# Seven chunks of weights instead of five have their bits assembled during attention

## The chip, the cores and the metric

The kernel runs on one core of a Trainium2 chip. The metric is the device time of one execution in microseconds. Before the change the median of 3 runs is 726.2 us (725.83 to 726.29).

## What is computed

Four batches of eight heads of attention over 576 positions, with a bias from a small MLP over relative positions, are followed by a feed-forward network (FFN) over the 2304 tokens.

```python
scores = scale * np.matmul(q, k.transpose(0, 1, 3, 2))
x = (psi_rel / psi_i)[..., None]
bias = np.maximum(x @ w1 + b1, 0.0) @ w2
scores = scores + bias.transpose(2, 0, 1)[None, :, :, :]
attn = softmax(scores)
x = (attn @ v).transpose(0, 2, 1, 3).reshape(B * S, H * D)
h = x @ w_in
out = np.maximum(0.01 * h, h) @ w_out
```

All inputs are float32 except the two weight matrices `w_in` (512 x 2048) and `w_out` (2048 x 512), which are float64. The kernel reads each of their elements as two 32-bit words and assembles a float32 from the bits.

## The kernel before

**Stages.** The bias is generated first (some 60 us). Then come 16 units of attention, one per pair of heads and batch, numbered 0 to 15; a unit has nine tiles, i = 0 to 8 (A0, B0, A1, B1, M, A2, B2, A3, B3), of 128 rows of scores each. Then the FFN runs over 4 blocks of 512 tokens and a last one of 256; in each block it goes through 16 chunks m of 128 hidden columns.

**Engines.** PE does all matmuls in float32r. `step(n)` issues tile n: its scores on PE (`qk_mm`, line 230) into one of two PSUM tiles `ps_s`, a DVE operation that adds the bias and takes the maximum (line 252), the transposes of the tile three before (line 295) and their evacuation on ACT (line 311), and the exponential on ACT (line 260). The context product of a unit's halves (`pv`, line 335) is issued in the steps i = 0 and i = 4 of the next unit. Its result is scaled on DVE (lines 344 and 348). For the first batch of each pair of heads, which belongs to FFN block 0, it is also split into a high and a low part: a cast on ACT (line 345) and a subtraction on DVE (line 360). These splits fall into units 1, 5, 9 and 13.

**Splits for float32r.** Each float32 operand is a high part (rounded by a copy into float32r) and a low part (the rest); three products make one. `split_hi` does it for q and k of the next unit on DVE (lines 192 and 197), `split_lo` the rest on GpSimd (POOL; lines 204 and 207).

**The weights.** Chunk m has two halves, one of `w_in` (called wi) and one of `w_out` (wo). A half passes through these functions:

- `w_fill` (line 394) loads its raw words into one of three buffers `raw` through SP's queue;
- `w_abs` (line 400, ACT) writes the high word without its sign into a tile `tmp`: **abs** below;
- `w_bits` k = 0 to 3 (DVE, lines 407, 409, 411, 413) clamps, shifts and masks, takes over the sign bits, and takes over three bits of the low word: **clamp, shift, sign, low** below. The last one frees the raw buffer and calls `w_fill`;
- `w_hi` (line 419, ACT) casts to the high part, and `w_lo` (line 423, DVE) subtracts it: **cast** and **residual**.

For chunks 0 to 4 abs to low are done during attention (for chunk 0 also cast and residual). A list `early_ops` is filled at n = 13, and from unit 2 on two of its operations are taken after the steps i = 0 and i = 4: **slot 0** and **slot 4** of a unit. The tiles `tmp` of chunks 0 to 2 rotate through four buffers in pool `stage`; chunks 3 and 4 have four more in `stage_y`.

```python
for _ in range({0: 2, 4: 2}.get(i, 0) if n >= 18 else 0):
    if early_ops:
        f, *args = early_ops.pop(0)
        f(*args)
```

**The FFN's work list.** The remaining weight work is in `todo`, each entry with a cost. In each FFN iteration j, `ffn1` of chunk j is issued on PE, then `work(2.6)`, then two activations on ACT (`ffn_act`, lines 449 and 450, into `gh` and `g`), `work(2.6)` again, the low part `gl` on DVE (`ffn_lo`, line 456), and `ffn2` of chunk j - 2 on PE (lines 467 to 469), whose third product per token tile reads `gl`. `work` takes entries until their costs reach its budget: clamp 0.42, shift 0.43, sign, low and residual 0.69 each, ACT's entries 0.

Of the kernel before, what the change touches and what calls it, by code (L numbers as in the profile page):

```python
# [8 lines left out]
F32 = mybir.dt.float32  # L9
# [6 lines left out]
DM, DFF = 512, 2048  # L16
# [3 lines left out]
MF = DFF // 128  # L20
HS = S // 2
S0 = 512 - HS
PIT = S + 32
KW = 2 * S + 64
KINDS = ["A0", "B0", "A1", "B1", "M", "A2", "B2", "A3", "B3"]
GEN = [16, 17] + list(range(16)) + [34, 35] + list(range(18, 26)) + list(range(33, 25, -1))
SPL = {0: [(0, "q")], 1: [(1, "q", 0)], 3: [(1, "q", 1)], 4: [(0, "k")], 5: [(1, "k", 0)], 7: [(1, "k", 1)]}
# [8 lines left out]
def attention_ffn(ctx: ExitStack, tc: tile.TileContext, qt, kt, vm, vt, wi, wo, cst, out):  # L36
    nc = tc.nc
    PS = bass.MemoryType.PSUM
    xp = ctx.enter_context(tc.tile_pool(name="xp", bufs=1))
# [10 lines left out]
    def pstile(tag):  # L50
        shape = [128, 1024] if tag == "s" else [128, 512]
        return ps.tile(shape, F32, tag=tag, name="ps_" + tag)

    raw_b = [[ap.tile([128, c], F32, name=f"raw{c}{i}") for c in (2 * S, KW)] for i in range(2)]
    ident = ap.tile([128, 128], F32, name="ident")
    make_identity(nc, ident[:])
# [131 lines left out]
    def split_hi(u, what):  # L188
        q_, k_ = raw[u]
        if what == "q":  # L190
            qs = qs_b[u % 2]
            nc.vector.tensor_copy(qs[:].rearrange("p (a c) -> p a c", a=2)[:, :, 0:S], q_[:].rearrange("p (a c) -> p a c", a=2))
            ks1 = ap.tile([128, KW], F32R, tag="ks1", name="ks1", bufs=2)
            ks2 = ap.tile([128, KW], F32R, tag="ks2", name="ks2", bufs=2)
            qk[u] = (qs, ks1, ks2)
# [3 lines left out]
    def split_lo(u, what, a):  # L199
# [5 lines left out]
        else:  # L205
            c = slice(S * a, KW if a else S)
            nc.gpsimd.tensor_sub(ks2[:, c], k_[:, c], ks1[:, c].bitcast(F32))
# [3 lines left out]
    def tile_id(n):  # L211
        u, i = divmod(n, 9)
        return u, KINDS[i]

# [21 lines left out]
    def softmax_a(n):  # L236
        u, kind = tile_id(n)
        hp = u // B
        bt = bias[hp, "M"][:] if kind == "M" else bias[hp, kind[1]][:, 0 if kind[0] == "A" else 1, :]
        col = 1 if kind[0] == "B" else 0  # L240
        if col == 0:
            mx_t[n] = ap.tile([128, 2], F32, tag="mx", name="mx", bufs=6)
            sm_t[n] = ap.tile([128, 4], F32, tag="sm", name="sm", bufs=6)
        else:
            mx_t[n], sm_t[n] = mx_t[n - 1], sm_t[n - 1]
        if kind == "M":
            pair[0] = ap.tile([128, S + 64], F32, tag="pM", name="pM", bufs=1)
        elif col == 0:
            pair[0] = ap.tile([128, 2 * S], F32, tag="p", name="p", bufs=3)
        p = pair[0][:, S * col:S * col + S]  # L250
        s_, i = st.pop(n), mx_t[n][:, col:col + 1]
        nc.vector.tensor_tensor_reduce(out=p, in0=s_[:, S0:S0 + S], in1=bt, scale=-0.125, scalar=3.4e38, op0=ALU.add, op1=ALU.min, accum_out=i)  # L252
        pp[n] = pair[0]
        ex_q.append((p, i, sm_t[n][:, col:col + 1]))
# [97 lines left out]
    def step(n):  # L352
        if n < NTILE:
            qk_mm(n)
            softmax_a(n)
        if 0 <= n - 1 < NTILE and KINDS[(n - 1) % 9][0] != "A":
            recip(n - 1)
# [12 lines left out]
    pools = {}  # L370
# [25 lines left out]
            nxt[0] += 1  # L396

    def w_abs(m, i):
        y = pools["y" if m in (3, 4) else "s"].tile([128, DM], F32, tag="tmp", name="tmp", bufs=4)
        nc.scalar.activation(out=y[:], in_=raws[m, i][:, :, 1].bitcast(F32), func=AF.Abs)  # L400
        tmps[m, i] = y

# [76 lines left out]
    with tc.manual_schedule():  # L479
        gen_setup()  # L480
        for u in range(2):
            load_unit(u)
            load_v(u)
        sp_ops = [(u, w, a) for u in range(1) for w, a in (("q", None), ("q", 0), ("q", 1), ("k", None), ("k", 0), ("k", 1))]
        done = -1
        early_ops = []
        for n in range(NTILE + LAG + 6):
            u, i = divmod(n, 9)
            if u == 0:
                while done < GEN_AT[i]:  # L490
                    gen_tick(done)
                    done += 1
                    if done >= 6 and done % 2 == 0 and sp_ops:
                        w = sp_ops.pop(0)
                        split_hi(*w[:2]) if w[2] is None else split_lo(*w)
            if n == 8:
                gen.close()
                early = ctx.enter_context(tc.tile_pool(name="early", bufs=1, side="right"))
                x_alloc(early, 0)
                w_alloc(early, 0)  # L500
                early.tile([128, 24], F32, name="gap")
                stage, stage_y = ExitStack(), ExitStack()
                pools["s"] = stage.enter_context(tc.tile_pool(name="stage", bufs=1, side="right"))
                pools["y"] = stage_y.enter_context(tc.tile_pool(name="stage_y", bufs=1, side="right"))
            step(n)
            if n == 13:
                w_fill()
                for m in range(5):
                    early_ops += [(w_abs, m, h) for h in range(2)]
                    early_ops += [(w_bits, m, h, k) for k in range(4) for h in range(2)]  # L510
                    if m == 0:
                        early_ops += [(w_hi, 0, h) for h in range(2)] + [(w_lo, 0, h, nc.vector) for h in range(2)]
            for _ in range({0: 2, 4: 2}.get(i, 0) if n >= 18 else 0):
                if early_ops:
                    f, *args = early_ops.pop(0)
                    f(*args)
            if n == NTILE + 2:
                ffn1(0, 0)
            if u < HP * B:
                if u % B == B - 1 and u // B + 1 < HP:  # L520
                    c = {1: "0", 2: "1", 3: "M", 4: "2", 6: "3"}.get(i)
                    if c:
                        load_bias(u // B + 1, c)
                if u + 1 < HP * B:
                    for f, *args in SPL.get(i, ()):
                        (split_hi, split_lo)[f](u + 1, *args)
                if i == 0 and u + 2 < HP * B:
                    load_unit(u + 2)
                if i == 8 and u + 2 < HP * B:
                    load_v(u + 2)  # L530
        att.close()
        fp = ctx.enter_context(tc.tile_pool(name="ffn", bufs=1, reuse_waits="tile"))
        for m in range(1, MF - 1):
            w_alloc(fp, m)
        for c in ("g", "gh", "gl"):
            gt[c] = [fp.tile([128, BLK], F32 if c == "g" else F32R, name=f"{c}{i}") for i in range(1 if c == "g" else 3)]
        w_split(1)

        def more():
            stage_y.close()  # L540
            w_alloc(ctx.enter_context(tc.tile_pool(name="last", bufs=1, reuse_waits="tile")), MF - 1)

        todo = []
        for m in range(2, 5):
            todo += [(0, w_hi, m, i) for i in range(2)] + [(0.69, w_lo, m, i, nc.vector) for i in range(2)]
        todo.append((0, more))
        halves_ = [(m, i) for m in range(5, MF) for i in range(2)]
        todo += [(0, w_abs, *t) for t in halves_[:2]]
        for j, t in enumerate(halves_):
            todo += [(0.42, w_bits, *t, 0), (0.43, w_bits, *t, 1)]  # L550
            if j:
                todo.append((0.69, w_lo, *halves_[j - 1], nc.vector))
            todo += [(0.69, w_bits, *t, 2), (0.69, w_bits, *t, 3)]
            todo.append((0, w_hi, *t))
            if j + 2 < len(halves_):
                todo.append((0, w_abs, *halves_[j + 2]))
        todo.append((0.69, w_lo, *halves_[-1], nc.vector))

        def work(budget):
            while todo and budget > 0:  # L560
                cost, f, *args = todo.pop(0)
                f(*args)
                budget -= cost

        seq = [(n, m) for n in range(len(BLOCKS)) for m in range(MF)]
        for j in range(len(seq) + 2):
            if j < len(seq):
                n, m = seq[j]
                if j:
                    ffn1(n, m)  # L570
                work(2.6)
                ffn_act(n, m)
                work(2.6)
                ffn_lo()
                if (n, m) == (0, MF - 3):
                    assert not todo
                    stage.close()
                    lp = ctx.enter_context(tc.tile_pool(name="late", bufs=1, side="right", reuse_waits="tile"))
                    x_alloc(lp, 1)
                    x_split(1, 0)  # L580
                if n + 1 < len(BLOCKS) and m >= MF - (4 if n else 3):
                    x_split(n + 1, m - MF + 4)
            if j >= 2:
                ffn2(*seq[j - 2])
# [41 lines left out]
```

## Time and profile before

| | us |
|---|---|
| median of 3 runs | 726.2 |
| the profiled execution | 725.89 |
| its span | 723.7 |
| PE busy | 703.4 (97%) |
| DVE busy | 394.2 (54%) |
| ACT busy | 365.7 (51%) |
| POOL busy | 127.0 (18%) |

A matmul counts as busy from its start to its modelled end, and matmuls overlap, so PE's share is an upper view of its work. An idle stretch is shown in brackets with what ended it. Instructions that follow each other closely on one engine and line are merged into one row with their count. The granted clock of TensorE is 1.00 of 2.4 GHz nearly throughout.

### The profile page before, as it was taken

The numbers are of one execution on the slowest core, as the hardware profiler recorded it, in microseconds if no ns is written. First come the engines' busy times: TensorE is split into PE (matmuls) and PEld (weight loads), VectorE is DVE, ScalarE is ACT, GpSimd is POOL, SyncE is SP. The second block draws the span as 40 slices with busy tenths as digits, with TensorE's granted clock in tenths as the row PEclk, the third lists the DMA queues.
The fourth block names the chain that finished last, engine by engine and source line by source line (L and its number), as shares of the span: only waits on it lengthen the run. The fifth ranks groups of instructions, "written<-read, shape, count | busy, mean of one in ns | idle before, by whom it ended". The sixth has DMA issues, their size and how long they took to land.

```text
span 723.7 us, 11398 instructions
## 1 busy us (share of the span) xinstructions
PE 703.4 (97%) x4192; PEld 556.7 (77%) x4192; DVE 394.2 (54%) x1012; ACT 365.7 (51%) x808; POOL 127.0 (18%) x167
## 2 busy tenths in 40 slices
PE   6899999999999999998999999999999999999998
PEld 2347788778877887776777888888888888888996
DVE  7997789789888889759998211112111221112111
ACT  7797777777868677764555231132221231122221
POOL 2104545445544444300000000000000000000000
PEclk9999999999999999999999999999999999999999
DMA  9798848537626960103552010000100010000100
GB/s 222 241 314 244 224 109 242 129 88 216 188 69 164 249 172 18 59 1 120 175 175 83 1 58 1 1 0 1 58 1 1 0 59 1 0 1 0 59 1 30
DMA packets 30263, 68.26 MB, mean 94 GB/s; under 512 B 8192, under 2 KB 8320, under 8 KB 30208
## 3 DMA queue, kind: packets, MB, share of 16 engines
q1 hardware_dynamic: 30208, 67.54, 32.9%
q8 instruction: 33, 0.54, 0.3%
q14 instruction: 22, 0.18, 0.1%
HBM read 51.92 MB, written 15.61 MB: 93 GB/s over the span
## 4 chain that ended last, share of the span: by engine, by line
PE 80%; DVE 16%; issue 1%; DMA 1%; ACT 1%; SPq 0%; DVEq 0%
PE ps_o L441 11%; PE ps_t L441 11%; PE ps_o L335 10%; PE ps_s L230 10%; PE ps_s L469 8%; PE ps_s L467 8%; PE ps_s L468 8%; PE ps_t L295 7%; DVE p L252 2%; PE ps_o L123 2%; DVE tmp L411 2%; PE ps_t L123 2%; DVE tmp L413 2%; DVE r L112 2%; DVE wol L423 1%
## 5 line engine op out<-in xcount | busy, mean ns | idle before, releaser
L456 DVE TENSOR_TENSOR gl<-g,gh 128x512 fp32r<-128x512 f32 (+1 forms) x80 | 51.0, 638 | 263.9 <-ACT g L450 263.9
L230 PE MATMUL ps_s<-ks,qs 128*128 128x288 f32 x640 | 120.2, 314 | 3.1 <-DVE mx L252 3.1
L469 PE MATMUL ps_s<-woh,gl 128*128 128x512 f32 x288 | 112.9, 392 | 1.9 <-DVE gl L456 1.9
L467 PE MATMUL ps_s<-woh,gh 128*128 128x512 f32 x288 | 112.5, 390 | 1.6 <-ACT g L450 1.6
L468 PE MATMUL ps_s<-wol,gh 128*128 128x512 f32 x288 | 112.3, 390 | 0.0
L252 DVE CUSTOM_DVE_ANT_0 p<-ps_s,bias 128x576 f32<-128x576 f32 x128 | 95.0, 751 | 24.3 <-PE ps_s L230 23.6
L260 ACT ACTIVATE p<-p,mx 128x576 f32<-128x576 f32 x128 | 99.9, 780 | 11.3 <-DVE mx L252 10.4
L230 PEld LDWEIGHTS ps_s<-ks,qs 128*128 128x128 f32 x640 | 89.4, 189 | 18.8 <-DVE mx L252 5.0
L311 ACT COPY PT<-ps_t 128x512 f32<-128x512 f32 x128 | 73.7, 576 | 37.5 <-PE ps_t L295 37.5
L449 ACT ACTIVATE gh<-ps_o 128x512 fp32r<-128x512 f32 (+1 forms) x39 | 21.5, 552 | 124.4 <-PE ps_o L441 124.4
L295 PE MATMUL ps_t<-ident,p 128*128 128x128 f32 x512 | 76.9, 273 | 0.9 <-ACT PT L311 0.8
L449 ACT ACTIVATE gh<-ps_t 128x512 fp32r<-128x512 f32 (+1 forms) x39 | 21.5, 552 | 111.1 <-PE ps_t L441 111.0
L335 PE MATMUL ps_o<-PT,v 128*64 128x288 f32 x512 | 69.2, 412 | 0.0
L469 PEld LDWEIGHTS ps_s<-woh,gl 128*128 128x128 f32 x288 | 54.0, 188 | 16.2 <-DVE gl L456 5.0
L467 PEld LDWEIGHTS ps_s<-woh,gh 128*128 128x128 f32 x288 | 54.2, 188 | 12.6 <-ACT g L450 2.0
L295 PEld LDWEIGHTS ps_t<-ident,p 128*128 128x128 f32 x512 | 61.7, 140 | 2.7 <-ACT PT L311 1.8
L468 PEld LDWEIGHTS ps_s<-wol,gh 128*128 128x128 f32 x288 | 54.2, 188 | 10.6
L441 PE MATMUL ps_t<-xh,wil 128*128 128x512 f32 (+1 forms) x156 | 57.3, 367 | 0.0
L441 PE MATMUL ps_o<-xh,wil 128*128 128x512 f32 (+1 forms) x156 | 57.3, 367 | 0.0
L441 PE MATMUL ps_t<-xl,wih 128*128 128x512 f32 (+1 forms) x156 | 57.3, 367 | 0.0
L441 PE MATMUL ps_o<-xl,wih 128*128 128x512 f32 (+1 forms) x156 | 57.3, 367 | 0.0
L441 PE MATMUL ps_o<-xh,wih 128*128 128x512 f32 (+1 forms) x156 | 57.3, 367 | 0.0
(98 smaller groups left out, 1114.5 us busy)
## 6 DMA issues: line engine op xcount, KB each, us to landing
raw<-kt SPq DMA_DIRECT2D x32, 304.0 KB, 5.8
raw<-qt SPq DMA_DIRECT2D x32, 288.0 KB, 5.2
raw<-wi SPq DMA_DIRECT2D x16, 512.0 KB, 3.6
raw<-wo SPq DMA_DIRECT2D x16, 512.0 KB, 3.6
scr<-x SPq DMA_DIRECT2D x21, 295.5 KB, 4.0
bias<-scr SPq DMA_DIRECT2D x16, 288.0 KB, 5.3
out<-x SPq DMA_DIRECT2D x18, 256.0 KB, 2.1
v<-vm SPq DMA_DIRECT2D x16, 256.0 KB, 4.1
```

Of the source, the lines that this page charges most:

```text
L230: nc.tensor.matmul(s_[:, S0 + HS * hh:S0 + HS * hh + HS], qs[:, c0:c0 + 128], ks[:, k0 + HS * hh:k0 + HS * hh + HS], start=(j == 0), stop= ...
L252: nc.vector.tensor_tensor_reduce(out=p, in0=s_[:, S0:S0 + S], in1=bt, scale=-0.125, scalar=3.4e38, op0=ALU.add, op1=ALU.min, accum_out=i)
L260: nc.scalar.activation(out=p, in_=p, func=AF.Exp, bias=i, scale=-1.0, accum_out=sm)
L295: nc.tensor.transpose(t0[:, 128 * jb:128 * jb + 128], p[:, p0 + 128 * jb:p0 + 128 * jb + 128], ident[:])
L311: nc.scalar.copy(out=PT[u, g][:, 0:8, c].rearrange("p (j h) c -> p j h c", h=2)[:, :, h, :], in_=t0[:].rearrange("p (j c) -> p j c", j=4))
L335: nc.tensor.matmul(o[64 * h:64 * h + 64, 0:HS], l, r, start=(jb == 0), stop=(jb == 4))
L441: nc.tensor.matmul(h_[:, :N], w, x[:, :N], start=(j == 0), stop=(j == len(mms) - 1))
L449: nc.scalar.activation(out=gh[:, :N], in_=h_[:, :N], func=AF.Prelu, alpha=0.01)
L456: nc.vector.tensor_sub(gl[:, :N], g[:, :N], gh[:, :N].bitcast(F32))
L467: nc.tensor.matmul(o, gh[:, c], wt[m][2][:], start=(m == 0), stop=False)
L468: nc.tensor.matmul(o, gh[:, c], wt[m][3][:], start=False, stop=False)
L469: nc.tensor.matmul(o, gl[:, c], wt[m][2][:], start=False, stop=(m == MF - 1))
```

## The change

The number of chunks whose bits are assembled during attention goes from 5 to 7. Their four additional tiles are allocated in a pool that lasts (`xp`), named `y50` to `y61`; the room is taken from the area for dynamic DMA descriptors, 2048 bytes per partition in place of the default. The slots take three operations each. In the FFN's list the casts and residuals of chunks 5 and 6 stand where those of chunks 2 to 4 do, ahead of the first abs, which is now that of chunk 7.

```diff
+EARLY = 7
...
+    tmp_x = {(m, i): xp.tile([128, DM], F32, name=f"y{m}{i}") for m in range(5, EARLY) for i in range(2)}
...
     def w_abs(m, i):
-        y = pools["y" if m in (3, 4) else "s"].tile([128, DM], F32, tag="tmp", name="tmp", bufs=4)
+        if (m, i) in tmp_x:
+            y = tmp_x[m, i]
+        else:
+            y = pools["y" if m in (3, 4) else "s"].tile([128, DM], F32, tag="tmp", name="tmp", bufs=4)
...
-                for m in range(5):
+                for m in range(EARLY):
...
-            for _ in range({0: 2, 4: 2}.get(i, 0) if n >= 18 else 0):
+            for _ in range({0: 3, 4: 3}.get(i, 0) if n >= 18 else 0):
...
-        for m in range(2, 5):
+        for m in range(2, EARLY):
             todo += [(0, w_hi, m, i) for i in range(2)] + [(0.69, w_lo, m, i, nc.vector) for i in range(2)]
-        todo.append((0, more))
-        halves_ = [(m, i) for m in range(5, MF) for i in range(2)]
+            if m == 4:
+                todo.append((0, more))
+        halves_ = [(m, i) for m in range(EARLY, MF) for i in range(2)]
...
-    nc = bacc.Bacc("TRN2", target_bir_lowering=False, num_devices=1)
+    nc = bacc.Bacc("TRN2", target_bir_lowering=False, num_devices=1, dynamic_dma_scratch_size=2048)
```

What the slots hold, where it matters below:

| unit | slot 0 before | slot 0 now | slot 4 before | slot 4 now |
|---|---|---|---|---|
| 2 | abs abs | abs abs clamp | clamp clamp | clamp shift shift |
| 3 | shift shift | sign sign low | sign sign | low cast cast |
| 5 | residual residual | shift shift sign | abs abs | sign low low |
| 6 | clamp clamp | abs abs clamp | shift shift | clamp shift shift |
| 7 | sign sign | sign sign low | low low | low abs abs |
| 9 | shift shift | low low abs | sign sign | abs clamp clamp |
| 11 | clamp clamp | abs abs clamp | shift shift | clamp shift shift |
| 12 | sign sign | sign sign low | low low | low abs abs |
| 13 | abs abs | clamp clamp shift | clamp clamp | shift sign sign |
| 14 | shift shift | low low | sign sign | none |
| 15 | low low | none | none | none |

DVE's order at slot 0 of unit 7 before. L265 and L266 belong to the reciprocal of the row sums, L192 is the cast of q, L252 the softmax operation of the next tile.

```order
L265 TENSOR_SCALAR sm<-sm 128x2
L266 RECIPROCAL sm<-sm 128x2
L411 SCALAR_TENSOR_TENSOR tmp<-raw,tmp 128x512 x2
L192 CAST qs_96<-raw_78 128x2x576
L252 ISA p,mx<-ps_s,bias 128x576
```

The same place with the change; the source lines are 2 to 5 higher.

```order
L267 TENSOR_SCALAR sm<-sm 128x2
L268 RECIPROCAL sm<-sm 128x2
L416 SCALAR_TENSOR_TENSOR tmp<-raw,tmp 128x512 x2
L418 SCALAR_TENSOR_TENSOR tmp<-raw,tmp 128x512
L194 CAST qs_100<-raw_82 128x2x576
L254 ISA p,mx<-ps_s,bias 128x576
```

A low operation now stands between the two signs and the cast of q.

DVE's order at slot 4 of unit 13 before, where L197 is the cast of k.

```order
L252 ISA pM,mx<-ps_s,biasM 128x576
L252 ISA mx 128x1
L265 TENSOR_SCALAR sm<-sm 128x2
L266 RECIPROCAL sm<-sm 128x2
L407 TENSOR_SCALAR tmp<-tmp 128x512 x2
L197 CAST ks_3767<-raw_79 128x1216
L252 ISA p,mx<-ps_s,bias 128x576
```

And with the change; y_80 and y_81 are two of the four new tiles.

```order
L254 ISA pM,mx<-ps_s,biasM 128x576
L254 ISA mx 128x1
L267 TENSOR_SCALAR sm<-sm 128x2
L268 RECIPROCAL sm<-sm 128x2
L414 TENSOR_SCALAR y_81<-y_81 128x512
L416 SCALAR_TENSOR_TENSOR y_80<-raw,y_80 128x512
L416 SCALAR_TENSOR_TENSOR y_81<-raw,y_81 128x512
L199 CAST ks_3802<-raw_83 128x1216
L254 ISA p,mx<-ps_s,bias 128x576
```

Two clamps have become a shift and two signs.

DVE's order before the first `gl` of the FFN, before the change (the residuals wil and wol of chunk 4, then the bits of chunk 5).

```order
L423 TENSOR_TENSOR wil_4463<-tmp,wih_4462 128x512
L423 TENSOR_TENSOR wol_4465<-tmp,woh_4464 128x512
L407 TENSOR_SCALAR tmp<-tmp 128x512
L409 TENSOR_SCALAR tmp<-tmp 128x512
L411 SCALAR_TENSOR_TENSOR tmp<-raw,tmp 128x512
L456 TENSOR_TENSOR gl_4510<-g_4506,gh_4507 128x512
L413 SCALAR_TENSOR_TENSOR tmp<-raw,tmp 128x512
```

With the change, from the residuals of chunk 4 on.

```order
L428 TENSOR_TENSOR wil_4495<-tmp,wih_4494 128x512
L428 TENSOR_TENSOR wol_4497<-tmp,woh_4496 128x512
L428 TENSOR_TENSOR wil_4499<-y_78,wih_4498 128x512
L428 TENSOR_TENSOR wol_4501<-y_79,woh_4500 128x512
L461 TENSOR_TENSOR gl_4542<-g_4538,gh_4539 128x512
L428 TENSOR_TENSOR wil_4503<-y_80,wih_4502 128x512
L428 TENSOR_TENSOR wol_4505<-y_81,woh_4504 128x512
L412 TENSOR_SCALAR tmp<-tmp 128x512
```

Ahead of the first `gl` the residuals of chunk 5 have taken the place of three operations on its bits; the first clamp, of chunk 7, comes after the residuals of chunk 6.

## Rows read from the trace of the kernel before

**Rows 1.** Stretches: length, busy us of PE, PEld, DVE, ACT, POOL, then granted clock.
```profile
160.00:200.00 40.00, 40.00 (x322) 32.90 (x320) 33.94 (x104) 29.94 (x72) 19.72 (x26) 1.00 0.66 184
...
330.00:350.00 20.00, 18.31 (x79) 14.86 (x80) 19.66 (x39) 11.95 (x21) 0.00 (x0) 1.00 0.53 162
```

**Rows 2.** Timeline of PE: last matmuls of context products (start, us, engine, line, operation).
```profile
169.38 0.66 PE L335 MATMUL ps_o<-PT,vt 128*64 128x288 f32 x4
...
185.24 0.66 PE L335 MATMUL ps_o<-PT,vt 128*64 128x288 f32 x4
...
208.95 0.66 PE L335 MATMUL ps_o<-PT,vt 128*64 128x288 f32 x4
...
218.72 0.66 PE L335 MATMUL ps_o<-PT,vt 128*64 128x288 f32 x4
...
274.15 0.66 PE L335 MATMUL ps_o<-PT,vt 128*64 128x288 f32 x4
...
283.62 0.66 PE L335 MATMUL ps_o<-PT,vt 128*64 128x288 f32 x4
```

**Rows 3.** Timeline of DVE and PE, unit 7, slot 0 and after slot 4.
```profile
169.06 1.36 DVE L411 SCALAR_TENSOR_TENSOR tmp<-raw,tmp 128x512 int32<-128x512 int32 x2
170.34 0.75 DVE L192 CAST qs<-raw 128x1152 fp32r<-128x1152 f32 x1
171.01 0.75 DVE L252 CUSTOM_DVE_ANT_0 p<-ps_s,bias 128x576 f32<-128x576 f32 x1
...
172.14 0.76 PE L230 MATMUL ps_s<-ks,qs 128*128 128x288 f32 x4
...
178.39 0.76 DVE L252 CUSTOM_DVE_ANT_0 p<-ps_s,bias 128x576 f32<-128x576 f32 x1 [0.70 <-PE ps_s L230]
```

**Rows 4.** Who waited for whom, 310 to 400 us (us in total, times, longest).
```profile
PE ps_s L469 <- DVE gl L456: 1.9, 7, 0.6
```

**Rows 5.** Timeline of DVE and PE in the FFN's first block.
```profile
323.01 0.68 DVE L423 TENSOR_TENSOR wil<-tmp,wih 128x512 fp32r<-128x512 f32 x1
...
329.35 0.68 DVE L456 TENSOR_TENSOR gl<-g,gh 128x512 fp32r<-128x512 f32 x1
...
383.59 0.50 PE L469 MATMUL ps_s<-woh,gl 128*128 128x512 f32 x1 [0.23 <-DVE gl L456]
...
389.52 0.50 PE L469 MATMUL ps_s<-woh,gl 128*128 128x512 f32 x1 [0.20 <-DVE gl L456]
```

**Rows 6.** The chain that ended last, FFN (start, us, what).
```profile
392.08 2.72 PE ps_o L441 x12
```

**Rows 7.** Timeline of DVE and PE, slots of units 9 and 13.
```profile
202.53 0.76 DVE L252 CUSTOM_DVE_ANT_0 p<-ps_s,bias 128x576 f32<-128x576 f32 x1 [0.24 <-PE ps_s L230]
...
208.70 1.36 DVE L411 SCALAR_TENSOR_TENSOR tmp<-raw,tmp 128x512 int32<-128x512 int32 x2
...
209.54 0.79 PE L230 MATMUL ps_s<-ks,qs 128*128 128x288 f32 x4
...
210.69 0.74 DVE L252 CUSTOM_DVE_ANT_0 p<-ps_s,bias 128x576 f32<-128x576 f32 x1
...
273.91 0.84 DVE L407 TENSOR_SCALAR tmp<-tmp 128x512 f32<-128x512 f32 x2
...
274.66 0.78 DVE L197 CAST ks<-raw 128x1216 fp32r<-128x1216 f32 x1
274.74 0.79 PE L230 MATMUL ps_s<-ks,qs 128*128 128x288 f32 x4
...
275.57 0.76 DVE L252 CUSTOM_DVE_ANT_0 p<-ps_s,bias 128x576 f32<-128x576 f32 x1
```

**Rows 8.** Timeline of ACT: abs pair in unit 8, exponential in unit 9.
```profile
185.67 1.21 ACT L400 ACTIVATE tmp<-raw 128x512 f32<-128x512 f32 x2
...
208.76 0.77 ACT L260 ACTIVATE pM<-pM,mx 128x576 f32<-128x576 f32 x1
```

**Rows 9.** DMA issues on the page: name, queue, count, KB each, us to landing.
```profile
raw<-wi SPq DMA_DIRECT2D x16, 512.0 KB, 3.6
```

## Prediction

> **What bounds the kernel now.** I read the busy time of two stretches first. In 160 to 200 us, inside attention, PE is busy 40.00 of 40 us and DVE 33.94; in 330 to 350 us, inside the first FFN block, DVE is busy 19.66 of 20 us and PE 18.31 [rows 1]. So DVE looks full in the FFN and seems to have 15% to spare in attention, and the granted clock is 1.00 in both. The mean says nothing on where that spare time lies, so next come the PE rows that end each unit's context product (line 335), which mark the beat. From 169.38 to 185.24 us a plain unit takes 15.86 us [rows 2]. Its PE never waits, although four heavy weight operations stand in it. In units 5, 9 and 13, which also split x for the FFN (lines 344 and 360), the beat is longer: from the product in slot 4 to the next one 9.77 us pass in unit 9 (208.95 to 218.72) and 9.47 us in unit 13 (274.15 to 283.62) [rows 2].
>
> Then the slot itself. In unit 7 (slot 0) two sign operations start at 169.06 and the q cast behind them at 170.34, so one costs 0.64 us of DVE time; the next tile's softmax begins at 171.01, ends 0.75 us later at 171.76, and the score matmul that reuses its PSUM tile starts on PE at 172.14 [rows 3]. **The spare time behind a slot 0 with two heavy operations is thus 0.38 us**, less than one more. In slot 4 of the same unit the softmax sat idle for 0.70 us before 178.39 [rows 3]: there one more heavy operation fits.
>
> Last, the FFN. The low halves gl come after both work calls of an iteration, and PE waits for them: 1.9 us in 7 waits [rows 4]. The first gl starts at 329.35. PE's first matmul on a new gl starts at 383.59 and the next at 389.52, 5.93 us apart [rows 5], while PE alone needs 2.72 us per twelve matmuls [rows 6], 5.44 us for a chunk's 24. These chunks go by DVE's pace until the work list is empty.
>
> **What moves, and its price.** Four half chunks (two chunks, wi and wo) have their abs, clamp, shift, sign and low operations issued in attention instead of in the FFN. At 0.64 us for sign and low and 0.37 us for clamp and shift (two from 273.91 to 274.66 [rows 7]) that is 4 x 2.02 = 8.1 us of DVE, and 4 x 0.61 = 2.4 us of ACT (two abs take 1.21 [rows 8]). Casts and residuals of these chunks stay in the FFN. The raw loads keep their number; a reload is still issued by the low operation, one half unit (some 8 us) or more before the abs that reads it, and lands 3.6 us after its issue in the median [rows 9], so I cost the SP queue at nothing; if that cover failed, ACT would stand behind the abs, in order, with all its exponentials. The smaller descriptor area and the four new tiles change addresses only: nothing.
>
> The larger part is that every slot now takes three operations, in other groupings. Plain units first.
> - **Sign, sign, low in slot 0** of units 3, 7 and 12: 0.64 us more than the row shows against 0.38 us spare. PE is full and cannot make it up: 0.26 us, with semaphore and pipeline restart about 0.3 each, 0.9 in all.
> - **Abs, abs, clamp in slot 0** of units 2, 6 and 11: the clamp must wait for the first abs on ACT. In unit 8 the abs pair starts at 185.67, the first is done at about 186.28 [rows 8]; clamp 0.37 and q cast 0.67 (170.34 to 171.01 [rows 3]) put the softmax at 187.35. In unit 7 it could start as late as 171.01 + 0.38 = 171.39; one beat (15.86) on that is 187.25. About 0.1 over, 0.2 with restart: 0.6 in all, between 0 and 1.
> - All other plain slots hold 1.4 us or less in slot 0 and 2.0 or less in slot 4, within 1.28 + 0.38 and 1.28 + 0.70: nothing. ACT's single abs and its casts fill time in which it waits for PE.
>
> Units 5, 9 and 13 have no spare time, and here the rows give the rate. With 1.28 us in slot 4 unit 9's softmax started 1.15 us after its score matmuls (209.54 to 210.69), with 0.75 us in unit 13 it started at the earliest, 0.83 us (274.74 to 275.57) [rows 7]. So it is late by slot - 0.96 us, and 0.32 us of lateness cost 9.77 - 9.47 = 0.30 us of the beat: **one for one**.
> - Unit 13, slot 4: shift, sign, sign, 1.65 us for two clamps: 0.69 late.
> - Unit 5, slot 4: sign, low, low, 1.92 us for two abs: 0.96 late.
> - Unit 9, slot 4: abs, clamp, clamp for two signs. The abs stands behind the exponential that starts at 208.76 [rows 8]; by unit 8's pair, abs ends 0.77 + 0.61 after that, 210.14. The second clamp (0.37) and the k cast (0.70) follow, softmax at 211.3 in place of 210.69: 0.6 more, although DVE has less to do.
> - Their slots 0: unit 9's grows from two shifts (0.75) to two lows (1.28), with 0.24 us of waiting ahead of the softmax at 202.53 [rows 7] to absorb part: 0.3 late. Units 5 and 13 hardly change. Together 0.3.
>
> That is 2.55 for the three units. **Attention: 0.9 + 0.6 + 2.55 = 4.05 us lost.** Both ends: nothing, if every slot hides, and 8.1, if all added DVE time is exposed. I stay near the middle because most light slots have shown room. Units 14 and 15 lose their operations, which gives nothing back, since PE fills plain units anyway.
>
> **FFN: what comes back.** The work list is metered by DVE cost, 2.6 us a call, not by chunks. Eighteen halves instead of 22 do not make an iteration shorter; they make the list end earlier. Before, PE waits for the gl of chunks up to 10. After, the list ends early in iteration 10, so gl of chunk 9 is the last that binds: 5.93 - 5.44 = 0.49 us. Ahead of the first gl there are now ten residuals of 0.60 us from 323.01, so it starts at 329.0 instead of 329.35 [rows 5]: 0.3 us. **Gain 0.8 us**, between 0.5 and 1.3 (one more chunk). ACT no longer stands behind a wih cast that waits for DVE before the second gh, so PE gets ahead there, only to wait longer for the next gl.
>
> Sum: -0.8 + 4.05 = +3.25. On the profiled execution (span 723.7, 725.89 us in all) that is 729.15; the median of the runs is 0.3 above it, 726.2, which gives **729.5 us**.
>
> One rule of the Trainium skill would have it otherwise: the page "Perfetto Trace Analysis", section "Optimization Strategy", says that where the most-contended engine changes over time, interleaving the regimes may help. By that rule DVE's work belongs in attention and the time would be the first rival's. What rows 1 show agrees that the regimes differ; rows 3 show that the room is not where the work is put.
>
> **Rivals.**
> 1. *The slots hide* (same or slightly faster). The product of line 335 covers the third operation, as the 0.70 us of idle DVE in slot 4 suggests. Decisive is the spare time: were it over 0.64 us in slot 0 and could units 5, 9 and 13 make up on the way, attention would cost 0 to 2.2 and the time be 725.4 to 727.6. Against it stand the 0.38 us and the one-for-one rate. Chance 0.17.
> 2. *The FFN gains its whole wait* (faster). If two chunks ready early let PE run without any gl wait, 1.9 us [rows 4] and what restarts cost would come back, and with hidden slots the time would be 722 to 724.7. Against it: the gl stay behind work calls of unchanged length. Chance 0.05.
> 3. *The collisions spread* (slower still). One place: the third operation delays k or q casts, GpSimd's subtractions behind them, and so the next unit's scores; or a reload lands after its abs and ACT stalls. At 1.5 us in two or three units more the time would be 732 to 735. POOL is busy only in attention [rows 1]; in unit 7 the pair of signs still ran at 0.64 us each [rows 3]. Chance 0.08. The Trainium skill, page "SBUF — State Buffer", section "Summary: rules for kernel authors", says that a DVE operation with two SBUF inputs and a GpSimd operation that reads SBUF exclude each other: the one issued second waits for the first to finish. The moved sign and low operations have two such inputs, and by that rule the time would be this rival's if they met POOL's subtractions; no row shows such a meeting in a slot.
> 4. *The change does nothing to the order*: excluded by the orders shown.
>
> **Numbers.** A measurement here can tell about 0.2% (1.45 us) from no change. My case, 727.5 to 731.5, has 0.70, of which 0.01 ends within that bound. Slower: 0.69 + 0.08 = 0.77. Same: 0.17 + 0.01 = 0.18. Faster: 0.05. The range 726.6 to 731.8 leaves out rivals 2 and 3 and the faster half of rival 1, 0.2 in all.
>
> **What would show it.** In the new profile: a PE wait for the softmax of about 0.3 us after slot 0 of units 3, 7 and 12; beats from slot 4 of units 5, 9 and 13 of about 10.4, 10.4 and 10.2 us; attention ending some 4 us later; PE's wait for gl ending one chunk earlier, and the FFN about 0.8 us shorter from its first matmul to the end. Plain units that keep 15.86 us and special ones that keep theirs would prove me wrong and rival 1 right; no gl waits in the FFN, rival 2.

## Result and profile after

The changed kernel takes 729.8 us (median of 4 runs, 728.94 to 731.15) against 726.15 us (4 runs): a ratio of 1.0053, 95% interval 1.0035 to 1.007. **It is slower by some 0.5%, close to the forecast.** The profiled execution took 729.68 us, its span is 727.6 us.

Stretches of the kernel after: length, busy us of PE, PEld, DVE, ACT, POOL, then granted clock, the DMA engines' busy share and their GB/s.

```profile
160.00:200.00 40.00, 39.96 (x317) 32.64 (x316) 35.80 (x106) 30.30 (x74) 19.13 (x26) 1.00 0.67 176
330.00:350.00 20.00, 19.23 (x83) 14.89 (x82) 19.68 (x37) 11.38 (x21) 0.00 (x0) 1.00 0.36 105
```

Against [rows 1] DVE has 1.86 us more to do in 40 us of attention, with POOL hardly changed; in the FFN it is as full as before, and PE is busier by 0.92 us of 20. The means again hide the matter. It is in the PE rows that end the context products, now line 337 (timeline of PE, kernel after):

```profile
171.52 0.66 PE L337 MATMUL ps_o<-PT,vt 128*64 128x288 f32 x4
...
187.77 0.66 PE L337 MATMUL ps_o<-PT,vt 128*64 128x288 f32 x4
...
211.70 0.66 PE L337 MATMUL ps_o<-PT,vt 128*64 128x288 f32 x4
...
222.02 0.66 PE L337 MATMUL ps_o<-PT,vt 128*64 128x288 f32 x4
...
278.12 0.66 PE L337 MATMUL ps_o<-PT,vt 128*64 128x288 f32 x4
...
288.24 0.66 PE L337 MATMUL ps_o<-PT,vt 128*64 128x288 f32 x4
```

These are the same six products as [rows 2]. The beat of a whole unit from slot 0 of unit 7 is 16.25 us instead of 15.86 (187.77 - 171.52), from slot 4 of unit 9 10.32 instead of 9.77, from slot 4 of unit 13 10.12 instead of 9.47. Read through all 32 products, the beats differ from before in eleven places, each behind a slot to which the prediction gave a cost (for unit 5's slot 0, 0.07 us, next to none); every other beat agrees within 0.02 us, the first unit's aside.

Slot 0 of unit 7 in the kernel after (timelines of DVE and PE; it answers to [rows 3]):

```profile
171.19 1.37 DVE L416 SCALAR_TENSOR_TENSOR tmp<-raw,tmp 128x512 int32<-128x512 int32 x2
172.47 0.68 DVE L418 SCALAR_TENSOR_TENSOR tmp<-raw,tmp 128x512 int32<-128x512 int32 x1
173.07 0.75 DVE L194 CAST qs<-raw 128x1152 fp32r<-128x1152 f32 x1
173.74 0.75 DVE L254 CUSTOM_DVE_ANT_0 p<-ps_s,bias 128x576 f32<-128x576 f32 x1
...
174.79 0.74 DVE L254 CUSTOM_DVE_ANT_0 p<-ps_s,bias 128x576 f32<-128x576 f32 x1
...
174.55 0.79 PE L232 MATMUL ps_s<-ks,qs 128*128 128x288 f32 x4
...
175.59 1.33 PE L232 MATMUL ps_s<-ks,qs 128*128 128x288 f32 x8
```

Two signs and a low take 1.88 us (171.19 to 173.07), the q cast follows, the softmax ends at 174.49, and PE's score matmul starts right behind it, 0.06 us later, at 174.55. Before there was 0.38 us between the two. The next softmax ends at 175.53, and the next score matmul starts 0.06 us behind it again, at 175.59.

Slot 4 of unit 9 in the kernel after (timelines of DVE, ACT and PE; it answers to [rows 7, 8]):

```profile
211.43 0.41 DVE L412 TENSOR_SCALAR tmp<-tmp 128x512 f32<-128x512 f32 x1
212.94 0.43 DVE L412 TENSOR_SCALAR tmp<-tmp 128x512 f32<-128x512 f32 x1 [1.10 <-ACT tmp L405]
213.28 0.79 DVE L199 CAST ks<-raw 128x1216 fp32r<-128x1216 f32 x1
213.98 0.75 DVE L254 CUSTOM_DVE_ANT_0 p<-ps_s,bias 128x576 f32<-128x576 f32 x1
...
211.49 0.78 ACT L262 ACTIVATE pM<-pM,mx 128x576 f32<-128x576 f32 x1
...
212.25 0.65 ACT L405 ACTIVATE tmp<-raw 128x512 f32<-128x512 f32 x1
...
212.28 0.79 PE L232 MATMUL ps_s<-ks,qs 128*128 128x288 f32 x4
```

The second clamp stands idle for 1.10 us: its abs comes after the exponential on ACT and ends about 212.9. Behind the clamp stand the k cast and the softmax, which starts 1.70 us after its score matmuls (212.28 to 213.98), where it was 1.15. DVE lost the time by waiting, not by working.

The FFN of the kernel after: two rows of DVE, the last wait of PE for a gl, and that wait's line in the table of waits from 315 to 404 us (they answer to [rows 4, 5]).

```profile
327.62 0.68 DVE L428 TENSOR_TENSOR wil<-tmp,wih 128x512 fp32r<-128x512 f32 x1
...
333.64 0.69 DVE L461 TENSOR_TENSOR gl<-g,gh 128x512 fp32r<-128x512 f32 x1
...
388.00 0.50 PE L474 MATMUL ps_s<-woh,gl 128*128 128x512 f32 x1 [0.18 <-DVE gl L461]
```

```profile
PE ps_s L474 <- DVE gl L461: 2.1, 10, 0.3
```

The first gl comes 6.02 us after the first residual (6.34 before). PE still waits for gl in ten chunks; the last that binds is that of chunk 9, one earlier than before.

The three stages, for every kernel that was profiled, from the end row of the second context product, that of the last one, and the span (us):

| kernel | until the 2nd product | to the last product | to the end | span |
|---|---|---|---|---|
| before | 78.92 | 243.01 | 401.8 | 723.7 |
| after | 79.17 | 247.38 | 401.0 | 727.6 |
| e1 regrouped, five chunks | 81.09 | 246.08 | 401.7 | 728.9 |
| e2 addresses alone | 79.21 | 243.04 | 401.8 | 724.0 |
| e3 placed by cost | 79.15 | 242.52 | 401.1 | 722.8 |
| e4 placed, 2.0 us | 79.08 | 242.50 | 395.8 | 717.4 |
| e5 after, 2.0 us | 78.98 | 247.42 | 395.8 | 722.2 |
| e6 before, 2.3 us | 79.03 | 243.03 | 401.7 | 723.8 |
| e7 ladder | 78.65 | 244.80 | 401.8 | 725.2 |
| e8 five chunks, 2.6 and 2.0 us | 79.12 | 243.06 | 400.0 | 722.2 |
| e9 the same, placed by cost | 79.13 | 242.50 | 398.7 | 720.3 |

So the change costs 4.37 us in attention, gives back 0.7 in the FFN, and 0.25 lies ahead of its first slot. The question for the experiments is what in attention costs: the work, its grouping or the addresses; and why so little comes back in the FFN.

### The profile page after: what moved, and what is told of

Its sections match the earlier page's. It is cut to its first block, busy times and chain, and to the rows that moved or that the text cites. A ratio compares the mean times of both kernels' runs of the same rounds, so it can differ in the third digit from the quotient of the medians.

```text
span 727.6 us, 11388 instructions
## 1 busy us (share of the span) xinstructions
PE 705.7 (97%) x4192; PEld 556.5 (76%) x4192; DVE 393.0 (54%) x1012; ACT 365.6 (50%) x808; POOL 124.9 (17%) x167
## 4 chain that ended last, share of the span: by engine, by line
PE 71%; DVE 17%; DMA 7%; ACT 2%; issue 2%; SPq 1%; DVEq 0%
PE ps_o L446 11%; PE ps_t L446 11%; PE ps_s L474 8%; PE ps_s L472 8%; PE ps_s L473 8%; PE ps_o L337 7%; PE ps_s L232 7%; PE ps_t L297 4%; DVE p L254 3%; DMA raw<-qt 3%; DMA bias<-scr 2%; DVE tmp L418 2%; DVE tmp L416 2%; PE ps_o L125 2%; PE ps_t L125 1%
## 5 line engine op out<-in xcount | busy, mean ns | idle before, releaser
L206 POOL TENSOR_TENSOR qs<-raw,qs 64x576 fp32r<-64x576 f32 x32 | 45.7, 1429 | 67.9 <-issue 29.9
```

The costliest lines, as they stand in the source:

```text
L206: nc.gpsimd.tensor_sub(dst, q_[64:128, S * a:S * a + S], dst.bitcast(F32))
```

## Experiments

**Grouping without work (e1).** The kernel before, three operations a slot, five chunks.

```diff
-            for _ in range({0: 2, 4: 2}.get(i, 0) if n >= 18 else 0):
+            for _ in range({0: 3, 4: 3}.get(i, 0) if n >= 18 else 0):
```

> The kernel before with three operations a slot in place of two, and still five chunks, so no DVE work is added; the list simply ends in unit 10. My theory (the grouping of operations in the slots costs, not the amount of work): the beats of units 2, 3, 5, 6, 7 and 9 grow as in the changed kernel, by 0.28, 0.37, 0.98, 0.27, 0.38 and 0.77 us, 3.05 in all, and units 11 to 13 keep the times of before or better (unit 13 has no operations left); with the FFN as before the time is 728.7 to 729.2. Rival (8.1 us of added DVE work is what costs): no work is added, so 726.2 within 0.5.

Measured: 730.47 us (4 runs, 729.04 to 730.87), ratio 1.0049 (1.0034 to 1.0064). The products at slot 4 of unit 9 and slot 0 of unit 11, each with its successor:

```profile
213.62 0.66 PE L335 MATMUL ps_o<-PT,vt 128*64 128x288 f32 x4
...
223.94 0.66 PE L335 MATMUL ps_o<-PT,vt 128*64 128x288 f32 x4
...
239.80 0.66 PE L335 MATMUL ps_o<-PT,vt 128*64 128x288 f32 x4
...
247.41 0.66 PE L335 MATMUL ps_o<-PT,vt 128*64 128x288 f32 x4
```

10.32 us in unit 9, as in the changed kernel; 7.61 us from slot 0 of unit 11, where the list is empty and where the changed kernel has 7.87. All beats up to unit 9 are those of the changed kernel within 0.02 us and all later ones those of before; attention lost 3.07 us (246.08 - 243.01), 3.05 were expected. **Grouping costs, without one operation more.** The other 1.30 us of the changed kernel's 4.37 fall in units 11 to 13, which only the longer list reaches with slots of three. The time still lies 1.3 us above the expectation, and the table says where: 2.17 us before the second product, ahead of every slot. This run's rows there (timelines of DVE and PE, then stretches):

```profile
67.34 0.76 DVE L252 CUSTOM_DVE_ANT_0 p<-ps_s,bias 128x576 f32<-128x576 f32 x1 [2.03 <-DMA bias<-scr]
...
68.16 0.80 PE L230 MATMUL ps_s<-ks,qs 128*128 128x288 f32 x4 [2.00 <-DVE mx L252]
```

```profile
64.00:68.00 4.00, 2.17 (x19) 1.93 (x17) 1.97 (x4) 2.37 (x7) 1.86 (x3) 1.00 0.69 205
68.00:72.00 4.00, 3.84 (x20) 2.42 (x22) 2.92 (x14) 3.30 (x8) 2.09 (x3) 0.65 1.06 231
```

A part of the bias landed late, PE stood still for 2 us, and in the next 4 us the granted clock was 0.65. Why the transfer was late is open; the order up to there is that of before. Only this run has a trace. That the other three had the late transfer too is not shown: their mean clocks, 0.995 to 0.998, do not tell it, since runs of the kernel before at 0.997 took 725.44 to 726.34 us. The case for grouping rests on the beats.

**Addresses alone (e2).** Four unused tiles and the small descriptor area.

```diff
+    tmp_x = [xp.tile([128, DM], F32, name=f"y{k}") for k in range(4)]
...
-    nc = bacc.Bacc("TRN2", target_bir_lowering=False, num_devices=1)
+    nc = bacc.Bacc("TRN2", target_bir_lowering=False, num_devices=1, dynamic_dma_scratch_size=2048)
```

> The kernel before with the descriptor area of 2 KB and four tiles allocated but unused, so that all addresses move as in the change; the order of the work is that of before. My theory: 726.2 within 0.5 us, no beat changes. Rival (the smaller descriptor area or the new addresses cost part of the 3.7 us): 727.5 or more, with the added time spread over stages that the slots do not touch, such as the start of unit 2, which was 0.24 us later with the change.

Measured: 726.51 us (10 runs), ratio 1.0003 (0.9993 to 1.0013); no beat of attention differs by more than 0.02 us from unit 2 on. The room for the tiles cost nothing.

**The same work, placed (e3).** Seven chunks; a slot takes operations while their cost fits its room and no DVE operation follows an abs of its own half.

```diff
-            for _ in range({0: 3, 4: 3}.get(i, 0) if n >= 18 else 0):
+            room = (0.75 if u % B == 1 else {0: 1.41, 4: 1.93}[i]) if n >= 18 and i in (0, 4) and u <= HP * B else 0
+            acts, new = 0, set()
+            while early_ops and room:
+                f, m, h, *k = early_ops[0]
+                act = f in (w_abs, w_hi)
+                cost = 0 if act else 0.37 if f is w_bits and k[0] < 2 else 0.64
+                if cost > room or (acts == 2 if act else (m, h) in new) or (f is w_abs and ("low", 2 * m + h - 3) in new):
+                    break
...
```

> Seven chunks as in the change, with the same 8.1 us of DVE work in attention, but filled into the slots by cost: at most 1.41 us in slot 0 and 1.93 us in slot 4 of plain units, 0.75 us in units 1, 5, 9 and 13, no DVE operation behind an abs of its own slot. My theory (spare time is local, and there is room for the work where it fits): the loss of 4.4 us in attention is gone, the plain units keep 15.86 us and units 5 and 13 their times of before or less, the FFN gains 0.7 us as with the change: 724.5 to 726. Rival (added DVE work in attention costs wherever it stands): 728 or more.

Measured: 724.91 us (8 runs, 724.01 to 726.22), ratio 0.9981 (0.9971 to 0.9992). Its beat from slot 4 of unit 9:

```profile
208.99 0.66 PE L337 MATMUL ps_o<-PT,vt 128*64 128x288 f32 x4
...
218.46 0.66 PE L337 MATMUL ps_o<-PT,vt 128*64 128x288 f32 x4
```

9.47 us, better than the 9.77 of before, since unit 9 has 0.75 us at most. The 8.1 us of added DVE work cost nothing, and attention even gains 0.49 us: 0.30 here and 0.20 in unit 5. The FFN gains 0.7, as in the changed kernel. The rival that the work itself costs falls.

**Smaller work calls (e4, e5).** The placed kernel and the changed kernel, both calls at 2.0 us.

```diff
-                work(2.6)
+                work(2.0)
```

> As the placed kernel, with the budget of both work calls in the FFN at 2.0 us in place of 2.6, so that the list of the FFN, now shorter by 8.1 us, is spread to iteration 13 and DVE's load per iteration falls below the 5.44 us that PE needs. My theory (the gl waits and the 5.93 us beat come from work calls of unchanged length): PE's waits for gl vanish but for the first, the FFN gains some 4 to 5 us, 720 to 722. Rival (the weights are late instead: PE then waits for residuals or abs of later chunks as much as it did for gl): 724.5 to 727.

> The changed kernel, its slots untouched, with both work calls of the FFN at 2.0 us in place of 2.6. My theory (the two parts are independent: 4.4 us lost in attention by the grouping, some 5.3 us to be had in the FFN from a shorter list spread wider): attention ends as late as with the change, PE's waits for gl are gone, 729.8 - 5.3 = 724.5, between 723.5 and 725.5. Rival (the gain of the placed kernel with 2.0 us needs its placing, for instance because a later attention delays the weights): over 726.

Measured: e4 719.57 us (4 runs), ratio 0.9905 (0.989 to 0.992); e5 724.42 us (8 runs), 0.9977 (0.9966 to 0.9988). e5 is where my theory put it; e4 lies 0.4 us below its range, since 4 to 5 us were expected of the FFN and it gave 5.3. Both rivals fall. In e4's table of waits PE has none for gl. The stretch from 330 to 350 us of e4, and three of its gl (timeline of DVE):

```profile
330.00:350.00 20.00, 20.00 (x90) 16.56 (x89) 19.59 (x38) 10.77 (x20) 0.00 (x0) 1.00 0.41 133
```

```profile
327.47 0.69 DVE L461 TENSOR_TENSOR gl<-g,gh 128x512 fp32r<-128x512 f32 x1
...
332.00 0.68 DVE L461 TENSOR_TENSOR gl<-g,gh 128x512 fp32r<-128x512 f32 x1
...
336.73 0.69 DVE L461 TENSOR_TENSOR gl<-g,gh 128x512 fp32r<-128x512 f32 x1
```

The gl come 4.53 and 4.73 us apart instead of 5.93, ahead of PE's 5.44 us, and PE is busy throughout. DVE is as busy as it was (19.59 us): a full DVE as such does not hold PE up, the amount of work that stands ahead of each gl does. From the stage table the smaller calls give 5.2 to 5.3 us with either filling of the slots, so the two parts of the change add up independently.

**Are the two more chunks needed? (e6, e8, e9).** The kernel before with smaller calls: both at 2.3 us (e6); the second one at 2.0 (e8); e8 with the slots filled by the rule of e3 (e9). With both at 2.0 the longer list (by its own costs 6 x 0.69 + 22 x 2.92 = 68.4 us, 2 x 2.23 an iteration) would need more than 15 iterations and has 14.

```diff
                 ffn_act(n, m)
-                work(2.6)
+                work(2.0)
```

> The kernel before, five chunks and two operations a slot, with both work calls at 2.3 us in place of 2.6. At 2.0 us its list, longer by two chunks' bits, would not be done by iteration 13, where its buffers are handed on. My theory (DVE's load per iteration sets the beat): 4.6 us of entries and a gl of 0.68 make up to 5.3 us, just under PE's 5.44, but a call overshoots its budget by part of an entry, so I expect some beats of 5.44 and some longer ones and a gain of 1 to 4 us: 722 to 725; the seven chunks are then worth what is left to the placed kernel with 2.0 us at 719.6. Rival (seven chunks are needed for any gain in the FFN, since the residuals come late): 726.2 or more. Second rival (the budget alone does it all, the seven chunks nothing): 720 or less.

> The kernel before, five chunks and two operations a slot, with the second work call of an iteration at 2.0 us in place of 2.6 (at 2.3 the calls took the very same entries, because they take whole ones: 0.42 + 0.43 + 0.69 + 0.69 is 2.23, still under 2.3, and one more makes 2.92). Now an iteration has some 2.92 + 2.23 = 5.15 us of entries by the list's costs, at the measured durations (0.37, 0.37, 0.64, 0.64, 0.60) about 4.6, and with the gl 5.2 to 5.3, under PE's 5.44; the list still ends by iteration 13. Theory A (the beat is DVE's load per iteration, and the seven chunks are not needed for the gain): the waits for gl vanish or nearly so, 721 to 722.5. Theory B (with five chunks the list is too long, weights come late as the budget falls): 725 to 727.

> As the mixed kernel (five chunks, second call at 2.0 us), and the slots filled by cost as in the placed kernel, with the descriptor area as it was. If Theory A holds, the placing gives the 0.3 us of unit 9 and 0.2 us of unit 5 on top: 0.5 us below the mixed kernel, 720.5 to 722, and so within 1 to 2 us of the placed kernel with seven chunks at 2.0 us (719.6): the seven chunks as such are then worth under 2 us. If Theory B holds: 724.5 to 726.5.

e6 measured 726.47 us (10 runs, 725.7 to 728.99), ratio 1.0005 (0.9995 to 1.0016). It told nothing on its question: with whole entries 2.3 takes the same ones as 2.6, and every engine's order is that of before. It serves as a repeat of before.

e8 measured 724.25 us (5 runs), ratio 0.9967 (0.9954 to 0.998), e9 723.37 us (5 runs), 0.9961 (0.9947 to 0.9975). Both lie 1.4 to 1.8 us above the upper end of Theory A and below B. The waits for gl are gone as A says, but there is one of another kind. e8, timelines of ACT and PE, and a stretch:

```profile
330.91 0.62 ACT L419 CAST wih<-tmp 128x512 fp32r<-128x512 f32 x1 [4.24 <-DVE tmp L413]
...
332.49 0.58 ACT L450 ACTIVATE g<-ps_s 128x512 f32<-128x512 f32 x1
...
333.12 0.80 PE L467 MATMUL ps_s<-woh,gh 128*128 128x512 f32 x1 [2.33 <-ACT g L450]
```

```profile
330.00:335.00 5.00, 2.67 (x9) 1.81 (x7) 4.86 (x11) 2.78 (x5) 0.00 (x0) 0.76 0.37 111
```

e9, timeline of PE, and the same stretch:

```profile
332.58 0.50 PE L472 MATMUL ps_s<-woh,gh 128*128 128x512 f32 x1 [2.33 <-ACT g L455]
```

```profile
330.00:335.00 5.00, 2.67 (x12) 1.99 (x11) 4.90 (x11) 3.46 (x6) 0.00 (x0) 1.00 0.49 138
```

With five chunks the first cast of the FFN's own bits stands on ACT, in order, ahead of an activation that PE needs, and waits 4.24 us for DVE. PE loses 2.33 us in both. The kernel before has this wait as well (the same table as [rows 4]):

```profile
PE ps_s L467 <- ACT g L450: 1.6, 1, 1.6
```

There it costs little. PE, at 5.44 us a chunk behind gl that come every 5.93, makes the lost time up and from chunk 5 on waits for each gl again, so the pace of the work list still sets the end of the stage. With seven chunks that cast comes later, when PE has work in hand, and the wait stands in no table of a seven-chunk kernel. With smaller calls, where nothing else holds PE, the wait counts in full: e9's two runs without a fall of the clock took 722.12 and 722.24 us, 2.6 us more than e4's median. My expectation of under 2 us was too low. But e9 also keeps the first work call at 2.6 us, so the 2.6 us are not shown to be the two chunks' alone, and a five-chunk kernel with that cast moved was not tried.

**How much a slot hides (e7).** Five chunks, slots filled unevenly from a table.

```diff
+LADDER = {(2, 0): 2, (2, 4): 4, (3, 0): 4, (3, 4): 2, (4, 0): 2, (4, 4): 2, (5, 0): 2, (6, 0): 2, (6, 4): 4, (7, 0): 2, (7, 4): 3, (8, 0): 3, (8, 4): 2, (10, 0): 2, (10, 4): 4, (11, 0): 1, (11, 4): 3, (12, 0): 4, (12, 4): 2, (14, 0): 1, (14, 4): 1, (15, 0): 2}
...
-            for _ in range({0: 2, 4: 2}.get(i, 0) if n >= 18 else 0):
+            for _ in range(LADDER.get((u, i), 0)):
```

> The five chunks of the kernel before, in slots filled unevenly to measure how much each hides. In plain units: slot 0 of unit 3 holds sign, sign, low, low (2.56 us), slot 0 of unit 8 shift, sign, sign (1.65), slot 0 of unit 12 abs, abs, clamp, clamp; slot 4 of unit 6 sign, sign, low, low (2.56), slot 4 of unit 11 sign, low, low (1.92), slot 4 of units 2 and 10 clamp, clamp, shift, shift (1.50). With the change sign, sign, low (1.92) in slot 0 cost 0.37, not the 0.26 of my working. Theory A (the loss is slot minus 1.55 us, one for one): unit 3 +1.01, unit 8 +0.10, unit 12 +0.64, unit 6 slot 4 +0.58 (2.56 less 1.98), the other slots 0. Theory B (0.38 us is spare as the row said, and a late softmax costs 0.11 more for the restart): unit 3 +1.01, unit 8 0, the rest as A. Rival (PE makes part of it up, so that the loss flattens): unit 3 +0.4 to 0.6. Units 5, 9 and 13 have at most two light operations in slot 0 and none in slot 4, and should be at 7.84 and 9.46. Sum about +2, time 727.7 to 729.

Measured: 727.91 us (10 runs), ratio 1.0022 (1.0013 to 1.0031). The beats from slot 0 of units 3 and 12, the abs pair and the clamps of unit 12 (timelines of PE, ACT and DVE):

```profile
103.97 0.66 PE L336 MATMUL ps_o<-PT,vt 128*64 128x288 f32 x4
...
112.55 0.66 PE L336 MATMUL ps_o<-PT,vt 128*64 128x288 f32 x4
...
251.11 0.66 PE L336 MATMUL ps_o<-PT,vt 128*64 128x288 f32 x4
...
259.55 0.66 PE L336 MATMUL ps_o<-PT,vt 128*64 128x288 f32 x4
...
251.54 1.22 ACT L401 ACTIVATE tmp<-raw 128x512 f32<-128x512 f32 x2
...
252.23 0.99 DVE L408 TENSOR_SCALAR tmp<-tmp 128x512 f32<-128x512 f32 x2 [1.35 <-ACT tmp L401]
```

| slot | holds, us of DVE | beat | plain beat | loss | expected by A |
|---|---|---|---|---|---|
| unit 8, slot 0 | shift, sign, sign 1.65 | 7.72 | 7.60 | 0.12 | 0.10 |
| units 3, 7, 12 of the changed kernel | sign, sign, low 1.92 | 7.97 to 7.98 | 7.60 | 0.37 to 0.38 | 0.37 (A is drawn from it) |
| unit 3, slot 0 | sign, sign, low, low 2.56 | 8.58 | 7.60 | 0.98 | 1.01 |
| unit 6, slot 4 | sign, sign, low, low 2.56 | 8.58 | 8.27 | 0.31 | 0.58 |
| unit 11, slot 4 | sign, low, low 1.92 | 8.26 | 8.26 | 0 | 0 |
| unit 12, slot 0 | abs, abs, clamp, clamp | 8.44 | 7.60 | 0.84 | 0.64 |

Slot 0 follows Theory A: what goes beyond 1.55 us is lost nearly one for one. B's zero in unit 8 and the flattening in unit 3 fall. Two misses: slot 4 hides more than its row of idle time said, about 2.25 us; and the second clamp of unit 12 waits for the second abs, which ends 1.22 us after 251.54, so it costs 0.57 us more than one clamp (0.27), not its own 0.37.

## Why the prediction was right

| step | predicted | measured |
|---|---|---|
| sign, sign, low in slot 0 of units 3, 7, 12 | 0.3 each, 0.9 | 0.37, 0.38, 0.38: 1.13 |
| abs, abs, clamp in slot 0 of units 2, 6, 11 | 0.2 each, 0.6 | 0.28, 0.27, 0.27: 0.82 |
| slot 4 of units 5, 9, 13 | 0.96, 0.6, 0.69 | 0.91, 0.55, 0.65 |
| slot 0 of units 5, 9, 13 | 0.3 | 0.07, 0.22, 0.01: 0.30 |
| attention | 4.05 | 4.37 |
| first gl earlier | 0.3 | 0.32 |
| FFN in all | 0.8 | 0.7 |

- **The spare time.** Its place was right, its size 0.1 us too large. The prediction took the 0.38 us between the end of the softmax and the next score matmul [rows 3]; e7 and the changed kernel put the loss at slot - 1.55, which makes 0.27 us spare behind two signs. In unit 7 PE's score matmul came 3.03 us after the product's end row (171.52 to 174.55) where it was 2.76 (169.38 to 172.14), so it was held up by the expected 0.27 us, but the beat lost 0.38. The prediction allowed 0.04 us for the difference, as "semaphore and pipeline restart", for which it had no row. What it left out is the next softmax. Before (timelines of DVE and PE):

```profile
172.06 0.74 DVE L252 CUSTOM_DVE_ANT_0 p<-ps_s,bias 128x576 f32<-128x576 f32 x1
...
173.10 1.31 PE L230 MATMUL ps_s<-ks,qs 128*128 128x288 f32 x8
```

It ended at 172.80, 0.30 us ahead of the next score matmul; with the change PE starts 0.06 us behind it, as it does behind the first, so it is held up a second time. From the first score matmul to the next 1.04 us pass instead of 0.96. Of the 0.08 us 0.05 lie behind the transposes between the two (they start at 175.18, before at 172.74), where the second hold is; the other 0.06 of the 0.11 us are not explained by a row. Of the 0.32 us by which attention was undercounted 0.23 come from here and 0.22 from the clamps below; the slots 4 of units 5, 9 and 13 were overcounted by 0.14.

- **The clamp behind its abs.** Right, and at 0.27 a little dearer than the 0.2. e7's fourth operation shows that ACT sets the price, not DVE. (The sum for the softmax's start gives 187.32, not 187.35; it changes nothing.)
- **Units 5, 9 and 13.** The one-for-one rate, drawn from 0.30 us of beat for 0.32 us of lateness [rows 2, 7], held to 0.05 us for three fillings, the idle clamp of unit 9 included. For that clamp the prediction's own terms add up to 211.21, not 211.3, so to 0.52 us late; 0.55 was measured. The slots 0 agree only in their sum: 0.3 was meant for unit 9, which lost 0.22.
- **The FFN.** That the list is metered by cost and so does not shorten an iteration was the step that kept the forecast from rival 2. e4 and e5 show it from the other side: with the calls shortened the gain of 5.2 us appears at once. The prediction also had ACT's wait ahead of the second gh vanish and PE wait the longer for gl: the 1.6 us are gone, and the waits for gl went from 7 to 10, one for each of the chunks 0 to 9.
- **Rival 1**, the hidden slots, is what e3 makes true by another filling; it was wrong for this one. **Rival 3** did not show. POOL's subtractions did move with the cast of q (in unit 7 the first starts at 174.06, 2.54 us after the product's row, where it was 1.94), but no beat lost more than its own slot accounts for, and ACT waited for no reload in attention.
- **The addresses**: costed at nothing, and e2 shows nothing.

The rule of the Trainium skill that the prediction weighed (page "Perfetto Trace Analysis", section "Optimization Strategy": interleaving regimes with different limits may help) agrees with e3 and e4 and not with the changed kernel: 8.1 us of DVE work fit into attention for nothing, but only in the slots with room. The exclusion that the Trainium skill states (page "SBUF — State Buffer", section "Summary: rules for kernel authors") had no effect on the moved operations that a run here shows: in slot 0 of unit 7 the signs and the low still took 1.88 us for three. What does run beside them there is POOL's copy `rb`, of the reciprocals of the row sums: 0.60 us at 171.40, against 0.29 at 176.04, and the same 0.60 beside the two signs before the change, at 169.27 (spans on POOL are rough). That fits the rule, by which the one issued second waits; here it is POOL's, and no beat shows it.

Of the 3.65 us between the medians the attention's 4.37 and the FFN's -0.7 account for all; the 0.25 us ahead of unit 2 are within what other runs of an unchanged start show (78.65 to 81.09 in the table). That 729.5 came within 0.3 us of 729.8 is partly luck: on the profiled executions the change costs 3.79 us, not 3.25, and the four runs of the changed kernel alone spread from 728.94 to 731.15.

## What to carry to other kernels

Spare time belongs to a place: before work is moved onto an engine that is idle 15% of the time, read the gap between the end of what would be delayed and the start of what waits for it at each place, and fill by duration, not by count. An operation that waits for another engine delays whatever stands behind it, even where its own engine has less to do. And work that leaves a metered list gives back only what the meter is set to give: lower the budget in the same change (719.6 us against 724.9 for the same work).

## What was not expected of the hardware

A stall of PE of some 2 us can be paid twice, but need not be. After waits of 2.00 us (e1) and 2.33 us (e8) the granted clock fell: it was 0.65 and 0.76 in the 4 and 5 us that hold the restart, a mean between the full level of 2.4 GHz and the lower one of 1.2, and 1.00 again within 10 us. After the same wait of 2.33 us in e9's profile it stayed at 1.00. e8's runs divide accordingly: 722.39 and 722.43 us at a mean clock of 1.000, and 724.25 to 724.36 at 0.997 to 0.998; e9's are 722.12 and 722.24 at 1.000, and 723.37 to 723.70 at 0.997 to 0.998. So a lower mean clock goes with some 1.9 us more in e8 and 1.4 in e9; one run of each has a trace.

Where PE is not what the stage waits for, the fall cost nothing. The five-chunk kernels with calls of 2.6 us have the 1.6 us wait at the same place. Behind it the clock stayed at 1.00 in the profiles of before and e6 and fell in those of e2 and e7. e2, same stretch as above:

```profile
330.00:335.00 5.00, 2.98 (x8) 2.09 (x9) 4.90 (x10) 2.83 (x6) 0.00 (x0) 0.83 0.45 115
```

From the last product to the end all four take 401.7 to 401.8 us: the work list sets the pace there, and PE makes the loss up. Without traces the runs agree: those of the kernel before that were taken beside e1 to e4 took 725.44 to 726.34 us at 0.997, and 725.74 to 727.38 at 1.000. In the changed kernel PE's waits from 315 to 404 us are at most 0.5 us long, and the mean clock of its profile is 1.000. What decides whether the clock falls was not tried.
